# A recurrent attention and low-rank mixer kernel: transposes by the SyncE queue, the low-rank part in the MLP2 bank, two small loads later

## The chip, the cores and the metric

The kernel runs on one core of one Trainium2 chip. A core has TensorE (PE, with its weight loads PEld), VectorE (DVE), ScalarE (ACT), GpSimd (POOL) and SyncE (SP), and 16 DMA engines that work off what the queues hand them. The metric is the device time of one execution in microseconds (us), the median of the runs. The time before is 177.41 us, the median of 3 runs (176.12 to 177.9).

## The reference

For 4 batches of 8 heads, 768 steps and 48 columns a head, a gated recurrence runs over time and its output goes through a low-rank mixing over time and an MLP over the 384 columns:

```python
for t in range(S):
    state = alpha[:, :, t, :, None] * state + np.einsum('bhd,bhe->bhde', k[:, :, t], v[:, :, t])
    y[:, :, t] = np.einsum('bhd,bhde->bhe', q[:, :, t], state)
# x: y with the heads side by side, (batch, 768, 384)
xt = x.transpose(0, 2, 1)
h = xt @ U @ V                      # U: 768 x 32, V: 32 x 768, over time
u = x + h.transpose(0, 2, 1)
ch = np.maximum(u @ w_ch1, 0.0) @ w_ch2      # 384 -> 1536 -> 384
return u + ch
```

Inputs and output are float32; the kernel computes its matmuls in bfloat16.

## The kernel before, in words

Each batch is worked in six units (24 in all, numbered batch*6 + unit). For a unit, four tiles of 128 rows are loaded (alpha, k, q, v, 192 KB each). ScalarE takes the logarithm of alpha (lt), TensorE sums it over time with a triangular matrix (cum, `f_cum`), ScalarE makes exp of the sum and of its negative (aa, ai), and GpSimd or VectorE scales q and k with them (rq, rk, `f_scale`). TensorE transposes rk and rq (`f_tr`) into PSUM, ScalarE or VectorE copies them to SBUF (kT, qT, `f_ev`), TensorE multiplies them (the scores, `f_sc`), VectorE masks (pm), and TensorE makes the unit's y from pm and v and from qT and the state (`f_y`), which is copied into xb. The state itself is built from rk and rv (`f_d`, `f_st`).

Batches 0 and 1 are worked by `stage_pair`, which takes four heads and 256 rows in a unit, batches 2 and 3 by `stage_gla`, which takes all eight heads and 128 rows. Their loads differ too: 128x4x96 (L342) and 128x8x48 (L349), so 512 and 1024 contiguous pieces for the same bytes.

When a batch's xb is there, `stage_mix` multiplies it with U (L681), copies the result (utx), multiplies V with it (L712) and adds xb on VectorE (L713): u, in the tile ub. For the MLP, u has to stand transposed (uT). In batch 0 uT is made straight from xb and utx by L700 and L703 and the copy behind them, and L712 and L713 are done beside it for the last addition alone. In batches 1 to 3 TensorE transposes ub, two row blocks at a time (L722), and one copy brings them to uT.

`mlp1` multiplies uT with w1 (36 matmuls of 384 columns for each half of the batch, L749) and takes the maximum with 0 (L759, L761). `mlp2` multiplies that with w2 in three groups of four matmuls for each of six row blocks (L772), VectorE adds ub (L779), and SyncE stores the 128 rows (L780).

The order of all this is written by a planner, the class `Plan`. Each piece of work is added with its engines and a cost on each, what it reads and writes, and a priority (lower goes first); `run` walks a clock and always gives out the piece that can start first, among those that can start at the same time the one with the lowest priority. From that come each engine's instructions, in a fixed order that the chip follows; each instruction waits for what it needs and holds up what stands behind it in its engine's queue. All loads and stores are issued by SyncE's queue, in such an order too. MLP work has the priority of a unit that lies `LEAD` (3.0) units further on than its batch's end (`mlp_prio`). TensorE works with tiles of different shapes; a piece has a `mode` for it, and the planner adds 95 ns when the mode changes. The eight PSUM banks are a pool (`bank`), and so are the SBUF tiles: 36 for loads (`io`), 4 for rk, 3 for rq, 3 for kT, 4 for qT.

Two small loads, U (L305) and V (L306), are cast by GpSimd and V is spread to four row groups (vm_sb); they have priority 2.5. Until 28 us TensorE also gets matmuls on a tile of zeros (L291) where it has nothing to do.

Of the kernel before, what the change touches and what calls it, by code (L numbers as in the profile page):

```python
# [40 lines left out]
class Plan:  # L41
# [47 lines left out]
    def run(self):  # L89
# [10 lines left out]
        while todo:  # L100
# [79 lines left out]
def kernel(  # L180
# [31 lines left out]

    W2AT = 7.9
    PAIR = (0, 1)
    RES = (1, 1, 1, 0)
    P = Plan()
    nc.scalar.preload_act_table_set("natural_log_exp_and_others")
# [84 lines left out]
            nc.gpsimd.tensor_copy(dst, src)  # L302

    def small():
        P.add({"SP": 450.0}, lambda e: nc.sync.dma_start(u_in, moe_U.rearrange("(c p) r -> p c r", p=128)), w=["u_in"], prio=2.5)  # L305
        P.add({"SP": 500.0}, lambda e: nc.sync.dma_start(v_in, moe_V), w=["v_in"], prio=2.5)  # L306
# [234 lines left out]
    def stage_gla(b, c, sprev, xb):  # L541
# [36 lines left out]
        tk, tq = Buf(bank), Buf(bank)  # L578
        kT, qT = Buf(kts), Buf(qts)

        def f_tr(ring, tb):
            t = bf(tb()).rearrange("p (e c) -> p e c", c=C)
            for p in range(HP):
                nc.tensor.matmul(  # L584
                    t[:, p, :],
                    lhsT=ring()[:, 2 * p : 2 * p + 2, :].rearrange("t h w -> t (h w)"),
                    rhs=ident, start=True, stop=True, is_transpose=True,
                )

        def f_ev(e, dst, tb):  # L590
            copy(e, dst(), bf(tb()).rearrange("p (e c) -> p e c", c=C)[:, 0:HP, :])

        P.add({"PE": mm(*[C] * 4)}, lambda e: f_tr(rk, tk), r=[rk], w=[tk], prio=pr + 18, slack=sl)
        P.add({"PE": mm(*[C] * 4)}, lambda e: f_tr(rq, tq), r=[rq], w=[tq], prio=pr + 18, slack=sl)
        P.add({"DVE": 335, "ACT": 500}, lambda e: f_ev(e, kT, tk), r=[tk], w=[kT], prio=pr + 8, slack=sl)
        P.add({"DVE": 335, "ACT": 500}, lambda e: f_ev(e, qT, tq), r=[tq], w=[qT], prio=pr + 8, slack=sl)

        sc = Buf(bank), Buf(bank)
        pm = Buf(pms)
# [73 lines left out]
    def stage_mix(b, xb, ub, uT):  # L673
# [19 lines left out]
        if b == 0:  # L693
            for tt in range(2):
                tb = [Buf(bank, 2) for _ in range(NCT)]
                cs = range(tt * NT, (tt + 1) * NT)

                def f_x(e, j, tb=tb, cs=cs):
                    for n, c in enumerate(cs):
                        nc.tensor.matmul(tb[j]()[:, n * C : (n + 1) * C], lhsT=xb()[:, c, j * C : (j + 1) * C], rhs=ident, start=(n == 0), stop=False, skip_group_check=True)  # L700

                def f_h(e, j, tt=tt, tb=tb):
                    nc.tensor.matmul(tb[j]()[:, 0:TW], lhsT=utx()[:, j * C : (j + 1) * C], rhs=vm_sb[:, tt * TW : (tt + 1) * TW], start=False, stop=True, skip_group_check=True)  # L703

                for j in range(NCT):
                    P.add({"PE": mm(*[C] * NT)}, lambda e, j=j, f=f_x: f(e, j), r=[x for c in cs for x in xk(b, xb, c)] + [(xb, NC - 2, 0)], w=[tb[j]], prio=pr + tt, slack=sl)
                    P.add({"PE": mm(TW)}, lambda e, j=j, f=f_h: f(e, j), r=[utx, ("vm", tt)], w=[tb[j]], prio=pr + tt, slack=sl)
                    P.add({"ACT": 390, "DVE": 470}, lambda e, j=j, tt=tt, tb=tb: copy(e, uT()[:, j, tt * TW : (tt + 1) * TW], tb[j]()[:, 0:TW]), r=[tb[j]], w=[(uT, tt, j)], prio=pr + tt, slack=sl)
            pr = mlp_prio(0, 0.3)
        for c in range(NC):  # L710
            hb = Buf(bank, 3 if b == 0 else 0)
            P.add({"PE": mm(DM)}, lambda e, c=c, hb=hb: nc.tensor.matmul(hb()[:, 0:DM], lhsT=vm_sb[:, c * C : (c + 1) * C], rhs=utx(), start=True, stop=True), r=[utx, ("vm", c // NT)], w=[hb], prio=pr + c, slack=sl)  # L712
            P.add({"DVE": 465}, lambda e, c=c, hb=hb: nc.vector.tensor_tensor(ub()[:, c, :], xb()[:, c, :], hb()[:, 0:DM], op=ALU.add), r=[hb] + xk(b, xb, c), w=[(ub, c)], prio=pr + c, slack=sl)  # L713
            if c % 2 == 1 and b > 0:
                ub2 = Buf(bank)

                def f_tr(e, c=c, ub2=ub2):
# [13 lines left out]

                P.add({"DVE": 450, "ACT": 710}, f_ev, r=[ub2], w=[(uT, c // 2)], prio=pr + c, slack=sl)

    def mlp_prio(b, x):
        return ((b + 1) * NC + LEAD + x * NC) * 100.0

    def mlp1(b, uT, h1, tt):
        for jt in range(NJ):
# [2 lines left out]

            if b == 0:
                need = [(uT, tt, j) for j in range(NCT)]
            else:
                need = [(uT, 0), (uT, 1)] if tt == 0 else [(uT, 1), (uT, 2)]

# [15 lines left out]

            P.add({"ACT": 395, "DVE": 470}, g, r=[hb], w=[(h1, tt, jt)], prio=-100)

    def mlp2(b, ub, h1, c):
        hb = Buf(bank, RES[b])
        tt = c // NT
        for g in range(3):

            def f(e, g=g):  # L770
                for jt in range(4 * g, 4 * g + 4):
                    nc.tensor.matmul(  # L772
                        hb()[:, 0:DM], lhsT=h1()[:, jt, c * C : (c + 1) * C], rhs=w2_sb[:, jt, :],
                        start=(jt == 0), stop=(jt == NJ - 1),
                    )

            P.add({"PE": mm(*[DM] * 4)}, f, r=[(h1, tt, jt) for jt in range(4 * g, 4 * g + 4)] + [("w2", jt) for jt in range(4 * g, 4 * g + 4)], w=[hb], prio=mlp_prio(b, 0.5 + c / 12.0 + g / 36.0))
        ou = Buf(outs)
        P.add({"DVE": 468}, lambda e: nc.vector.tensor_tensor(ou(), ub()[:, c, :], hb()[:, 0:DM], op=ALU.add), r=[hb, (ub, c)], w=[ou], prio=-100)  # L779
        P.add({"SP": 550.0}, lambda e: nc.sync.dma_start(out[b, c * C : (c + 1) * C, :], ou()), r=[ou], prio=-1)  # L780

    small()
# [4 lines left out]
    for b in range(B):  # L787
        xb, ub, uT, h1 = Buf(xbs), Buf(ubs), Buf(uts), Buf(h1s)
        st = [None, None]
        for c in range(NC):  # L790
            if b in PAIR:
                st[c % 2] = stage_pair(b, c, st[c % 2], xb)
            else:
                st[0] = stage_gla(b, c, st[0], xb)
        stage_mix(b, xb, ub, uT)
        mlp1(b, uT, h1, 0)
        mlp1(b, uT, h1, 1)
        for c in range(NC):
            mlp2(b, ub, h1, c)
    P.run()  # L800
    global PLAN
    PLAN = P
# [30 lines left out]
```

## Time and profile before

| What | Value |
|---|---|
| Time, median of 3 runs | 177.41 us (176.12 to 177.9) |
| The profiled execution's time | 174.75 us |
| Its span, first to last instruction | 173.0 us |
| Granted TensorE clock, mean | 0.986 |
| TensorE busy | 161.9 us (94%), 1862 matmuls |
| VectorE, ScalarE, GpSimd busy | 109.0, 104.1, 59.5 us |
| Moved by DMA | 28.82 MB, 167 GB/s over the span |

Durations in the profile are of one execution, and busy time is the union of an engine's instructions. TensorE's matmuls overlap: the mean of one matmul is longer than the time by which one follows another, so the price of a matmul is read from the chain, where a row says how long a group of them took. A row of the SyncE queue tells how long the queue was held until the next transfer could be issued; the landing comes some us later.

### The profile page before, as it was taken

To read this page: it belongs to the slowest core of one execution; us is meant where nothing else is said; L and a number is where in the kernel's file an instruction comes from. 1 tells how busy PE (TensorE), PEld (TensorE's weight loads), DVE (VectorE), ACT (ScalarE), POOL (GpSimd) and SP (SyncE) were. 2 spreads that over 40 slices of the span, in tenths; PEclk is the share of its full clock that TensorE was granted. 3 is DMA by queue.
4 is the path that set the end of the run, shared out by engine and by line. 5 is a ranking of instruction groups with operands and counts; after the bars stand their busy time and mean duration, and the time that the engine had idled before them with its cause. 6 is when DMAs were issued, how large, how long until landed. Compare 5 with 4: busy or idle time off the path is not lost.

```text
span 173.0 us, 4823 instructions
## 1 busy us (share of the span) xinstructions
PE 161.9 (94%) x1862; PEld 104.2 (60%) x1862; DVE 109.0 (63%) x232; ACT 104.1 (60%) x247; POOL 59.5 (34%) x97
## 2 busy tenths in 40 slices
PE   7688998899996999999998999999999999999991
PEld 2355765566564776676676657666666566656560
DVE  4589685598996986958675559976474294000231
ACT  4588773779785767558949436638783210996000
POOL 8056366247331765255155414910430000000000
PEclk9999699999999999999999999999999999999998
DMA  5999989999998999999989999611000212100222
GB/s 140 266 249 260 267 255 335 258 300 330 269 267 200 178 207 211 214 222 221 230 147 206 189 166 258 170 58 37 0 0 4 91 45 91 51 0 0 91 93 91
DMA packets 83031, 28.82 MB, mean 167 GB/s; under 512 B 76832, under 2 KB 82976, under 8 KB 83008
## 3 DMA queue, kind: packets, MB, share of 16 engines
q1 hardware_dynamic: 83008, 28.52, 72.0%
q8 instruction: 14, 0.23, 0.6%
q14 instruction: 9, 0.07, 0.2%
HBM read 23.79 MB, written 4.72 MB: 165 GB/s over the span
## 4 chain that ended last, share of the span: by engine, by line
PE 60%; DMA 19%; SPq 15%; issue 2%; POOL 1%; ACT 1%; DVE 0%; ACTq 0%; POOLq 0%
PE ps L772 27%; PE ps L749 16%; SPq L342 10%; DMA io<-in_v_dram 8%; DMA io<-in_moe_w_ch_dram 5%; SPq L317 3%; DMA io<-in_alpha_dram 3%; PE ps L584 3%; DMA io<-in_k_dram 3%; PE ps L605 2%; PE ps L712 2%; PE ps L722 2%; PE ps L664 1%; PE ps L554 1%; PE ps L418 1%
## 5 line engine op out<-in xcount | busy, mean ns | idle before, releaser
L749 PE MATMUL ps<-uT,w_sb 128*128 128x384 bf16 x288 | 53.1, 326 | 0.0
L772 PE MATMUL ps<-w_sb,h1t 128*128 128x384 bf16 x288 | 52.8, 326 | 0.0
L759 ACT ACTIVATE h1t<-ps 128x384 bf16<-128x384 f32 x73 | 35.2, 494 | 8.8 <-PE ps L749 8.5
L772 PEld LDWEIGHTS <-h1t 128*128 128x128 bf16 x288 | 26.1, 98 | 16.0 <-issue 1.0
L749 PEld LDWEIGHTS <-w_sb 128*128 128x128 bf16 x288 | 26.1, 98 | 15.4
L779 DVE TENSOR_TENSOR ou<-ub,ps 128x384 f32<-128x384 bf16 x24 | 13.2, 551 | 27.6 <-PE ps L772 27.3
L302 POOL CAST rv<-io 128x384 bf16<-128x384 f32 x19 | 11.2, 590 | 35.7 <-DMA io<-in_v_dram 30.7
L615 DVE TENSOR_TENSOR pm<-ps,maskc 128x512 bf16<-128x512 f32 x24 | 15.7, 685 | 6.7 <-PE ps L605 6.5
L572 POOL TENSOR_TENSOR rk<-io,ai 128x384 bf16<-128x384 f32 x12 | 11.0, 916 | 20.2 <-ACT ai L565 18.7
L761 DVE TENSOR_SCALAR h1t<-ps 128x384 bf16<-128x384 f32 x23 | 12.6, 552 | 7.4 <-PE ps L749 4.8
L456 DVE TENSOR_TENSOR pm<-ps,maskp 128x512 bf16<-128x512 f32 x24 | 15.8, 681 | 0.7 <-ACT h1t L759 0.5
L298 ACT CAST xb<-ps 128x192 bf16<-128x192 f32 (+1 forms) x23 | 8.8, 392 | 11.6 <-PE ps L664 7.6
L298 ACT COPY kt<-ps 128x512 bf16<-128x512 bf16 x17 | 10.0, 586 | 5.8 <-PE ps L584 5.3
L713 DVE TENSOR_TENSOR ub<-xb,ps 128x384 bf16<-128x384 bf16 x24 | 12.1, 547 | 1.2 <-PE ps L712 1.2
L298 ACT COPY qt<-ps 128x512 bf16<-128x512 bf16 x17 | 11.3, 663 | 1.6 <-PE ps L418 1.0
L302 POOL CAST w_sb<-io 128x384 bf16<-128x384 f32 x21 | 10.8, 527 | 3.8 <-DMA io<-in_moe_w_ch_dram 3.5
L572 POOL TENSOR_TENSOR rq<-io,aa 128x384 bf16<-128x384 f32 x12 | 11.6, 967 | 0.0
L375 ACT ACTIVATE lt<-io 128x384 bf16<-128x384 f32 x12 | 6.4, 530 | 5.2 <-DMA io<-in_alpha_dram 5.2
L298 ACT COPY uT<-ps 128x768 bf16<-128x768 bf16 x4 | 3.2, 799 | 8.6 <-PE ps L722 5.1
L547 ACT ACTIVATE lt<-io 128x384 bf16<-128x384 f32 x12 | 6.5, 542 | 2.0 <-DMA io<-in_alpha_dram 2.0
L398 ACT ACTIVATE ai<-ps 128x384 bf16<-128x384 f32 x12 | 5.9, 493 | 2.8 <-PE ps L391 2.8
L565 ACT ACTIVATE ai<-ps 128x384 bf16<-128x384 f32 x12 | 6.0, 500 | 2.4 <-PE ps L557 2.0
(114 smaller groups left out, 249.3 us busy)
## 6 DMA issues: line engine op xcount, KB each, us to landing
io<-in_alpha_dram SPq DMA_DIRECT2D x24, 192.0 KB, 4.3
io<-in_k_dram SPq DMA_DIRECT2D x24, 192.0 KB, 4.5
io<-in_q_dram SPq DMA_DIRECT2D x24, 192.0 KB, 4.3
io<-in_v_dram SPq DMA_DIRECT2D x24, 192.0 KB, 4.5
io<-in_moe_w_ch_dram SPq DMA_DIRECT2D x24, 192.0 KB, 4.4
out_dram<-ou SPq DMA_DIRECT2D x24, 192.0 KB, 1.9
u_in<-in_moe_U_dram SPq DMA_DIRECT2D x1, 96.0 KB, 4.6
v_in<-in_moe_V_dram SPq DMA_DIRECT2D x1, 96.0 KB, 4.3
```

Source lines behind the costliest of these rows:

```text
L298: nc.scalar.copy(dst, src)
L302: nc.gpsimd.tensor_copy(dst, src)
L342: lambda e: nc.sync.dma_start(t().rearrange("p (h j) d -> p h (j d)", j=2), src[b, hs, sl, :].rearrange("h (p j) d -> p h (j d)", j=2)),
L456: nc.vector.tensor_tensor(dst, s2, maskp.to_broadcast([C, 2, 2, C]), op=ALU.mult)
L572: eng.tensor_tensor(dst()[:, :, 0:D], a(), x(), op=ALU.mult)
L615: nc.vector.tensor_tensor(pm()[:, :, par, :], s2, maskc.to_broadcast([C, HP, C]), op=ALU.mult)
L713: P.add({"DVE": 465}, lambda e, c=c, hb=hb: nc.vector.tensor_tensor(ub()[:, c, :], xb()[:, c, :], hb()[:, 0:DM], op=ALU.add), r=[hb] + xk( ...
L749: nc.tensor.matmul(hb()[:, 0:TW], lhsT=w1_sb[:, ct, jt * 128 : (jt + 1) * 128], rhs=uT()[:, ct, tt * TW : (tt + 1) * TW], start=(ct == 0), ...
L759: nc.scalar.activation(dst, hb()[:, 0:TW], AF.Relu)
L761: nc.vector.tensor_scalar_max(dst, hb()[:, 0:TW], 0.0)
L772: nc.tensor.matmul(hb()[:, 0:DM], lhsT=h1()[:, jt, c * C : (c + 1) * C], rhs=w2_sb[:, jt, :], start=(jt == 0), stop=(jt == NJ - 1),)
L779: P.add({"DVE": 468}, lambda e: nc.vector.tensor_tensor(ou(), ub()[:, c, :], hb()[:, 0:DM], op=ALU.add), r=[hb, (ub, c)], w=[ou], prio=-100)
```

## The change

In words:

- In batches 2 and 3 rk and rq are no longer transposed by TensorE. SyncE issues a transposing DMA from the rk or rq tile to the kT or qT tile (`TRD = (2, 3)`), with priority -0.5, so ahead of the loads that are ready at the same time. The transposes' PSUM banks and the two copies fall away.
- In batch 3 each row block of ub is transposed by such a DMA as well (`TRU = (3,)`), one of 128x384 for each of the six row blocks; L722's transposes and their copies remain for batches 1 and 2. `mlp1` then waits for the three row blocks of its half.
- In batch 0 `stage_mix` ends when uT is made. The low-rank product for the last addition is a thirteenth matmul in each row block's MLP2 bank, and the last addition reads xb in place of ub.
- The loads of U and V get priority 4.5 in place of 2.5.
- `LEAD` is 4.0 in place of 3.0, and a piece of TensorE work in another mode than the one before counts as 20 points lower in priority (`STAY`).

```diff
+    STAY = 20.0
-                t1, op = min(((t, o) for t, o in ok if t <= t0 + 1.0), key=lambda x: (x[1].prio, x[1].i))
+                t1, op = min(((t, o) for t, o in ok if t <= t0 + 1.0), key=lambda x: (x[1].prio + (self.STAY if eng == "PE" and x[1].mode != mode else 0.0), x[1].i))
...
+    TRD = (2, 3)
+    TRU = (3,)
...
-        P.add({"SP": 450.0}, lambda e: nc.sync.dma_start(u_in, moe_U.rearrange("(c p) r -> p c r", p=128)), w=["u_in"], prio=2.5)
-        P.add({"SP": 500.0}, lambda e: nc.sync.dma_start(v_in, moe_V), w=["v_in"], prio=2.5)
+        P.add({"SP": 450.0}, lambda e: nc.sync.dma_start(u_in, moe_U.rearrange("(c p) r -> p c r", p=128)), w=["u_in"], prio=4.5)
+        P.add({"SP": 500.0}, lambda e: nc.sync.dma_start(v_in, moe_V), w=["v_in"], prio=4.5)
...
-    LEAD = 3.0
+    LEAD = 4.0
...
+        if b in TRD:
+            for ring, dst in ((rk, kT), (rq, qT)):
+                P.add(
+                    {"SP": 600.0},
+                    lambda e, ring=ring, dst=dst: nc.sync.dma_start(dst(), ring().rearrange("t h w -> t (h w)"), transpose=True),
+                    r=[ring], w=[dst], prio=-0.5,
+                )
+        else:
...
-            pr = mlp_prio(0, 0.3)
+            return utx
...
-            if c % 2 == 1 and b > 0:
+            if b in TRU:
+                P.add(
+                    {"SP": 450.0},
+                    lambda e, c=c: nc.sync.dma_start(uT()[:, :, c * C : (c + 1) * C], ub()[:, c, :], transpose=True),
+                    r=[(ub, c)], w=[(uT, c)], prio=-0.5,
+                )
+            elif c % 2 == 1:
...
+            low = b == 0 and g == 2
...
-                        start=(jt == 0), stop=(jt == NJ - 1),
+                        start=(jt == 0), stop=(jt == NJ - 1 and not low),
...
+                if low:
+                    nc.tensor.matmul(hb()[:, 0:DM], lhsT=vm_sb[:, c * C : (c + 1) * C], rhs=utx(), start=False, stop=True)
...
-        P.add({"DVE": 468}, lambda e: nc.vector.tensor_tensor(ou(), ub()[:, c, :], hb()[:, 0:DM], op=ALU.add), r=[hb, (ub, c)], w=[ou], prio=-100)
+        P.add({"DVE": 468}, lambda e: nc.vector.tensor_tensor(ou(), (xb if b == 0 else ub)()[:, c, :], hb()[:, 0:DM], op=ALU.add), r=[hb] + (xk(b, xb, c) if b == 0 else [(ub, c)]), w=[ou], prio=-100)
```

More of the change, by code (lines that the diff above doesn't have):

```diff
@@ L590, in f_ev, with f_tr @@
[L590 to L596, printed above, removed]
+        if b in TRD:
[4 more added lines that the diff above has]
+                    r=[ring], w=[dst], prio=-0.5,
+                )
+        else:
+            tk, tq = Buf(bank), Buf(bank)
+            def f_tr(ring, tb):
+                t = bf(tb()).rearrange("p (e c) -> p e c", c=C)
+                for p in range(HP):
+                    nc.tensor.matmul(
+                        t[:, p, :],
+                        lhsT=ring()[:, 2 * p : 2 * p + 2, :].rearrange("t h w -> t (h w)"),
+                        rhs=ident, start=True, stop=True, is_transpose=True,
+                    )
+            def f_ev(e, dst, tb):
+                copy(e, dst(), bf(tb()).rearrange("p (e c) -> p e c", c=C)[:, 0:HP, :])
+            P.add({"PE": mm(*[C] * 4)}, lambda e: f_tr(rk, tk), r=[rk], w=[tk], prio=pr + 18, slack=sl)
+            P.add({"PE": mm(*[C] * 4)}, lambda e: f_tr(rq, tq), r=[rq], w=[tq], prio=pr + 18, slack=sl)
+            P.add({"DVE": 335, "ACT": 500}, lambda e: f_ev(e, kT, tk), r=[tk], w=[kT], prio=pr + 8, slack=sl)
+            P.add({"DVE": 335, "ACT": 500}, lambda e: f_ev(e, qT, tq), r=[tq], w=[qT], prio=pr + 8, slack=sl)
@@ L743, in mlp1 @@
                 need = [(uT, tt, j) for j in range(NCT)]
+            elif b in TRU:
+                need = [(uT, c) for c in range(tt * NT, (tt + 1) * NT)]
             else:
```

21 lines of the change are left out of this document (7 added, 14 removed).

## The prediction

> **What bounds the kernel now.** I read the page first, then the engines by stage, then the waits of TensorE, the chain of waits, and last the issue times of the SyncE queue.
>
> ```profile
> span 173.0 us, 4823 instructions
> PE 161.9 (94%) x1862; PEld 104.2 (60%) x1862; DVE 109.0 (63%) x232; ACT 104.1 (60%) x247; POOL 59.5 (34%) x97
> DMA  5999989999998999999989999611000212100222
> PE 60%; DMA 19%; SPq 15%; issue 2%; POOL 1%; ACT 1%; DVE 0%; ACTq 0%; POOLq 0%
> ```
>
> Two resources are full, one after the other in the chain: the DMA engines until slice 25 of 40 (about 108 us), TensorE nearly all the time. A busy TensorE is not proof of a bound, so the stages come next. Columns are the busy time and the instruction count of each engine, then the granted clock, the DMA share and GB/s.
>
> ```profile
> 0.00:36.00 36.00, 30.55 (x441) 19.45 (x442) 24.69 (x67) 24.05 (x59) 17.40 (x40) 0.95 1.03 256
> 56.00:88.00 32.00, 32.00 (x432) 21.63 (x431) 25.21 (x49) 23.22 (x57) 16.67 (x22) 1.00 1.06 210
> 92.00:110.00 18.00, 18.00 (x204) 12.06 (x203) 13.12 (x26) 11.37 (x31) 8.78 (x12) 1.00 1.22 208
> 110.00:146.00 36.00, 36.00 (x352) 23.21 (x350) 22.23 (x41) 16.55 (x37) 6.63 (x8) 1.00 0.13 45
> ```
>
> And what TensorE waited for between 36 and 170 us:
>
> ```profile
> PE ps L479 <- POOL rv L302: 1.5, 1, 1.5
> PE ps L605 <- ACT qt L298: 0.6, 1, 0.6
> ```
>
> So from 36 us on TensorE waits 2.1 us in all, and what leaves its queue there shortens the span; before 36 us the loads set the pace. VectorE and ScalarE are not waited for beyond 0.6 us. The chain of waits gives prices on the bounding engine (start, duration, line and number of instructions):
>
> ```profile
> 63.97 0.45 PE ps L584 x8
> 64.42 0.65 PE ps L772 x4
> ...
> 65.92 0.33 PE ps L605 x8
> 66.25 0.76 PE ps L772 x4
> ...
> 70.63 0.34 PE ps L722 x6
> ...
> 146.10 11.70 PE ps L749 x72
> 157.80 11.71 PE ps L772 x72
> 169.54 0.55 DVE ou L779
> ```
>
> A transpose costs TensorE 0.45/8 = 56 ns (L584) or 0.34/6 = 57 ns (L722). Four MLP2 matmuls take 0.65 us, but 0.76 us behind L605, which uses another tile shape: a change of shape costs 0.11 us. The last batch's MLP is 23.4 us of full-rate matmuls.
>
> **What leaves TensorE.** On TensorE, where the first unit of batch 2 (rk_154, rv_171) is worked, stood in the kernel before:
>
> ```order
> L628 MATMUL ps<-rv_171,rk_154 128x96
> L628 LDWEIGHTS rk_154
> L628 MATMUL ps<-rv_171,rk_154 128x96
> L584 LDWEIGHTS rk_154
> L584 MATMUL ps<-ident,rk_154 128x128
> L584 LDWEIGHTS rk_154
> L584 MATMUL ps<-ident,rk_154 128x128
> ```
>
> and now (L639 is the old L628, L800 the low-rank matmul that joins an MLP2 bank, L521 the old L518 of the unit before):
>
> ```order
> L795 MATMUL ps<-w_sb,h1t_211 128x384
> L800 LDWEIGHTS vm_sb
> L800 MATMUL ps<-utx_206,vm_sb 128x384
> L639 LDWEIGHTS rk_154
> L639 MATMUL ps<-rv_171,rk_154 128x96
> L639 LDWEIGHTS rk_154
> L639 MATMUL ps<-rv_171,rk_154 128x96
> ```
>
> The transposes behind the state matmuls are gone. 12 units x 2 tensors x 4 = 96 transposes at 56 ns are 5.3 us; batch 3's 18 of u at 57 ns are 1.0 us. Batch 0's six low-rank matmuls stay, as L800 in place of L712: nothing. Changes of tile shape fall from 100 to 92 when counted over the order: at most 8 x 0.11 = 0.9 us, part of it in the load-bound start, and I take 0.4. Together 6.7 us off TensorE: span 173.0 - 6.7 = **166.3 us** if nothing new waits.
>
> Off the path, at nothing: 24 copies of kT and qT, 3 copies of uT and 6 additions of u leave ScalarE and VectorE, which are covered by TensorE's work; if that cover were gone, the 0.6 us wait above is what they could give. Batch 0's final addition reads xb where it read ub, at the same price. U and V move behind eight loads:
>
> ```profile
> 8.37 0.68 SPq L305 DMA_DIRECT2D u_in<-in_moe_U_dram  x1
> 9.10 1.05 SPq L306 DMA_DIRECT2D v_in<-in_moe_V_dram  x1
> ...
> L681 PE MATMUL ps<-xb,u_sb x24: 322/336/337, 23.4 to 137.2; 128*32 128x384 bf16 x24
> ```
>
> The eight loads issue 1.7 us earlier, the two small loads near 15 us, 8 us ahead of U's first use at 23.4; what comes behind them keeps its place, so I take nothing (between 0.7 gained and 0.7 lost, the shorter of the two issue times). MLP rows stand one unit further back (LEAD), and the mode bonus reorders a little: same work, and the one place where TensorE waits for a load (L479, 1.5 us) may close or double, so 1.5 either way, taken as nothing.
>
> **What goes into the DMA queue.** 24 transposes of 128 KB and 6 of 96 KB now stand in SyncE's queue. Around the first of them stood before:
>
> ```order
> L780 DMA out_0_dram<-ou0_213 128x384
> L349 DMA io4_116<-in_alpha_dram 128x8x48
> L349 DMA io9_121<-in_k_dram 128x8x48
> L349 DMA io11_123<-in_q_dram 128x8x48
> L349 DMA io6_118<-in_v_dram 128x8x48
> L780 DMA out_0_dram<-ou1_214 128x384
> ```
>
> and now:
>
> ```order
> L352 DMA io9_121<-in_k_dram 128x8x48
> L805 DMA out_0_dram<-ou1_214 128x384
> L352 DMA io11_123<-in_q_dram 128x8x48
> L586 DMA_TRANSPOSE kt0_188<-rk0_154 128x4x128
> L586 DMA_TRANSPOSE qt0_184<-rq0_151 128x4x128
> L352 DMA io6_118<-in_v_dram 128x8x48
> L805 DMA out_0_dram<-ou2_215 128x384
> ```
>
> Each transpose waits on SyncE for GpSimd's rk or rq; behind it queue loads of later units and the outputs, and GpSimd's casts and ScalarE's Ln wait for those. At the end of the loads the queue read, before:
>
> ```order
> L349 DMA io6_118<-in_k_dram 128x8x48
> L780 DMA out_0_dram<-ou3_216 128x384
> L349 DMA io12_124<-in_q_dram 128x8x48
> L349 DMA io15_127<-in_v_dram 128x8x48
> L780 DMA out_0_dram<-ou0_213 128x384
> ```
>
> and now:
>
> ```order
> L586 DMA_TRANSPOSE qt1_185<-rq0_151 128x4x128
> L352 DMA io11_123<-in_q_dram 128x8x48
> L352 DMA io6_118<-in_v_dram 128x8x48
> L586 DMA_TRANSPOSE kt1_189<-rk2_156 128x4x128
> L586 DMA_TRANSPOSE qt2_186<-rq1_152 128x4x128
> L586 DMA_TRANSPOSE kt2_190<-rk3_157 128x4x128
> L586 DMA_TRANSPOSE qt3_187<-rq2_153 128x4x128
> ```
>
> 20 of the 24 transposes now stand ahead of the last load. No row shows such a transpose; its price T on a full queue comes from the queue's own rows (start, time until the next could issue):
>
> ```profile
> 18.98 7.24 SPq L317 DMA_DIRECT2D io<-in_moe_w_ch_dram  x12
> ...
> 39.99 1.25 SPq L342 DMA_DIRECT2D io<-in_k_dram  x1
> ...
> 53.27 0.57 SPq L349 DMA_DIRECT2D io<-in_alpha_dram  x1
> ...
> 61.72 1.07 SPq L780 DMA_DIRECT2D out_dram<-ou  x1
> ...
> 105.29 0.64 SPq L780 DMA_DIRECT2D out_dram<-ou  x1
> ...
> 106.50 0.69 SPq L349 DMA_DIRECT2D io<-in_v_dram  x1
> ```
>
> All these move 192 KB. Weights, 128 rows of 384 numbers, take 7.24/12 = 0.60 us. The sixteen loads from 39.99 to 53.27 come in 512 pieces (128x4x96): 0.83 us. From 53.27 to 107.19 there are 48 loads in 1024 pieces (128x8x48) and 8 outputs (61.72 to 105.29); with the outputs at the weights' 0.60, a load is (53.92 - 4.8)/48 = 1.02 us. By the first and the last of these a piece costs 0.42 us/896 = 0.47 ns and the bytes alone 0.54 us (for the middle one that makes 0.78, measured 0.83). A transpose moves two thirds of the bytes and writes 128x4 pieces of 256 bytes: 0.36 + 512 x 0.47 ns = **0.60 us, an estimate**. The lower end is 128 pieces, 0.42 us; the upper end, as long as a whole L349 load, 1.02 us. I take 0.60, since its piece count is that of the middle rows.
>
> The Trainium skill speaks against the change here: "VectorE: DVE Perf Modes", section "The three transpose paths", gives a 128x128 transpose 390 ns on TensorE and 1309 ns by DMA, and advises TensorE where PSUM will do. The chain's 56 ns already undercuts the first figure; by the second, four blocks in turn would be an estimated 5.2 us and 20 of them some 92 us more.
>
> With T = 0.60 the issue of the last load, which ended at 106.50 + 0.69 = 107.19, ends at 107.19 + 4 more outputs x 0.60 + 20 x 0.60 = 121.6 us. From there the shortest way to the end has these rows, of the last unit and the last mix before:
>
> ```profile
> DMA to landing us min/median/max: 3.2/4.2/5.5
> ...
> out_dram<-ou SPq DMA_DIRECT2D x24, 192.0 KB, 1.9
> ...
> 128.92 0.91 POOL L572 TENSOR_TENSOR rq<-io,aa 128x384 bf16<-128x384 f32 x1
> ...
> 132.31 0.40 PE L605 MATMUL ps<-qt,kt 48*128 48x128 bf16 x8
> ...
> 135.41 0.36 PE L664 MATMUL ps<-rv,pm 128*128 128x48 bf16 x8
> ...
> 137.01 0.50 PE L681 MATMUL ps<-xb,u_sb 128*32 128x384 bf16 x6
> ...
> 138.75 1.14 PE L712 MATMUL ps<-utx,vm_sb 128*128 128x384 bf16 x6
> 139.12 2.41 DVE L713 TENSOR_TENSOR ub<-xb,ps 128x384 bf16<-128x384 bf16 x5 [0.26 <-PE ps L712]
> ```
>
> Before, the last rq ran at 128.92, some 18 us after its load: the loads had slack. Now: issued 120.9 + 4.2 landing = 125.1; rq 0.9 and a gap of 0.1: 126.1; its transpose on a queue that has run empty 1.9 + 0.6 = 2.5: 128.6; L605 to L664 3.1, to L681 1.6, to L712 1.7 as in the rows: 135.0; three additions of u (0.4 until the first starts, then 3 x 0.5): 136.9; transpose of the third row 1.9 + 0.45 (384 pieces, half the bytes): 139.3; and from the start of the last MLP1 to the end as before, 173.0 - 146.10 = 26.9: **166.2 us**. Both paths end together, so a little is lost where they meet. Before, one wait for qt cost 0.6; now every unit has such a wait through the queue. I add two of these, 1.2 us (bounds 0 and, at a third of a us in each of 12 units, 4). Span **167.5 us**.
>
> **The rivals.** *The queue becomes the bound, slower.* Each 0.05 us on T moves the end by 1.0 us. The change is lost at span 173.0, T = 0.60 + 5.5/20 = 0.88; it is over 1% slower from T = 0.97. At 1.02 the span is 166.2 + 8.4 + 1.2 = 175.8 us. For it: DMA is full until 108 us, and no row shows a transpose. Against: its bytes and pieces are fewer than an L349 load's. 0.15.
>
> *Four transfers in one, much slower.* If the queue works each 128-column block as a transfer of its own, at the 0.60 us of the shortest transfer in the rows, T is 2.4 and the span 167.5 + 20 x 1.8 = 203.5 us. Nothing in the trace speaks for it but that no such transfer is in it. The page on VectorE named above would put it higher still. 0.04.
>
> *The gain turns into waits.* With T between 0.79 and 0.97, or 4 us of waits at the units, loads arrive just as TensorE has run out of MLP rows, and the span is 171.2 to 174.8. 0.14.
>
> *The waits that are there go too.* If T is at the lower end, the loads reach the end 3.6 us earlier, and with the 2.1 us of waits gone and the whole 0.9 us of shape changes won the span is 166.3 - 2.1 - 0.5 = 163.7 us. 0.07.
>
> **How the numbers follow.** My forecast has 0.60, which leaves 0.67 for faster by over 1%. The profiled execution took 174.75 us, 1.75 beyond its span and 2.66 below the median of 177.41; I keep both distances, so a span s stands for s + 4.4. Forecast: 167.5 gives 169.25 profiled and **171.9 us**. The range runs from the third rival, 163.7 (168.1), to T = 1.02, 175.8 (180.2). 1% of 177.41 is 1.8 us, about what a measurement of this kernel can tell from no change: 175.6 and 179.2 are the spans 171.2 and 174.8 used above.
>
> **What would show it.** L584 gone, L739 (the old L722) at 36 matmuls; TensorE's waits from 36 us on near 3 us, for kt and qt landing; the last L352 load issued near 121 us rather than 106.5; a transpose of 0.6 us in a full queue, landing in 4.2 us there and about 2.5 at the end; the last MLP1 starting near 140 us. Wrong if the last load issues after 127 us, or if TensorE stands idle ahead of L616 for over 0.5 us per unit.

## The result, and the profile after

The changed kernel is slower: 182.72 us (median of four runs, 181.11 to 183.44) against 176.76 us (175.75 to 177.9) for the kernel before on the same chip, a ratio of 1.032 with a 95% interval of 1.022 to 1.042. The forecast was 171.9 us, its range ended at 180.2: the sign was wrong, and the range did not hold the time. Some executions of a kernel take over 1.5% longer than its fastest; the ratios leave them out, the medians do not. The profiled execution of the changed kernel took 182.83 us, of which the span is 181.0; before it was 173.0, so 8.0 us are to be found.

The page of the changed kernel begins like this; the last line is the DMA queue (packets, MB, share of 16 engines).

```profile
span 181.0 us, 4585 instructions
PE 157.2 (87%) x1746; PEld 98.7 (55%) x1749; DVE 102.1 (56%) x215; ACT 93.8 (52%) x223; POOL 62.2 (34%) x105
DMA  4999999999999997899899998998889314410222
PE 39%; DMA 28%; SPq 17%; POOL 5%; ACT 4%; issue 3%; DVE 2%; POOLq 0%; ACTq 0%; DVEq 0%
q1 hardware_dynamic: 98560, 32.26, 84.1%
```

The instructions did leave TensorE: 1862 recorded matmuls became 1746 and its busy time fell by 4.7 us. But the DMA engines, empty from about 108 us on before, are now busy until slice 31 of 40 (140 us), and in the chain TensorE's share fell from 60% to 39% while DMA rose from 19% to 28%. TensorE's waits of the changed kernel between 36 and 178 us (line waited for: us in total, times, longest) say where the saving went:

```profile
PE ps L616 <- DMA qt<-rq: 4.7, 8, 1.2
PE ps L557 <- ACT lt L550: 4.5, 6, 1.5
PE ps L639 <- POOL rv L305: 1.6, 3, 0.7
PE ps L770 <- DMA uT<-ub: 1.6, 1, 1.6
PE ps L616 <- ACT h1t L780: 0.6, 1, 0.6
```

These are 13.0 us where there were 2.1. Two kinds stand out: the score matmuls (L616) wait for the transposed q, and the cumulative sums (L557) wait for ScalarE's Ln of alpha. The second is a late load. In the waits of all engines, ScalarE's wait for alpha's load was 2.0 us in the kernel before (first row) and is 17.2 in the changed one (second row):

```profile
ACT lt L547 <- DMA io<-in_alpha_dram: 2.0, 4, 1.4
```

```profile
ACT lt L550 <- DMA io<-in_alpha_dram: 17.2, 12, 3.7
```

What made the loads late is seen in the SyncE queue of the changed kernel (start, duration, line and operation). A duration here is the time for which the instruction holds SyncE's queue, not the time until the data has landed:

```profile
69.64 0.57 SPq L352 DMA_DIRECT2D io<-in_v_dram  x1
70.31 0.53 SPq L805 DMA_DIRECT2D out_dram<-ou  x1
70.94 1.24 SPq L586 DMA_TRANSPOSE kt<-rk  x1
72.27 1.22 SPq L586 DMA_TRANSPOSE qt<-rq  x1
...
133.53 0.57 SPq L352 DMA_DIRECT2D io<-in_v_dram  x1
136.91 1.21 SPq L586 DMA_TRANSPOSE kt<-rk  x1
138.21 1.22 SPq L586 DMA_TRANSPOSE qt<-rq  x1
```

The same by source, with the time from issue to landing of L586 (durations in ns, min/median/max):

```profile
L586 SPq DMA_TRANSPOSE kt<-rk x12: 1205/1242/2456, 65.8 to 136.9; - x12
L586 SPq DMA_TRANSPOSE qt<-rq x12: 1205/1214/1370, 68.4 to 138.2; - x12
...
DMA to landing us min/median/max: 2.4/3.3/5.4
...
L728 SPq DMA_TRANSPOSE uT<-ub x6: 1183/1206/1215, 149.1 to 157.0; - x6
```

A transposing instruction holds the queue for 1.2 us. It is the same at 70.94 in a full queue and at 136.91, when the last load has gone out and only transposes stand ahead; and the same for the 96 KB of L728 as for the 128 KB of L586. The load and the output shown beside it hold the queue 0.57 and 0.53 us. The 20 transposes ahead of the last load hold it 26.6 us in all by their rows, of which 20 x 1.21 = 24.2 are this hold, so waiting in the queue for GpSimd's rk and rq can be 2.4 us of it at most. The last load is issued by 133.53 + 0.57 = 134.1 us, where it was 107.19 before and 121.6 was forecast.

### The profile page after: what moved, and what is told of

Its sections match the earlier page's. It is cut to its first block, busy times and chain, and to the rows that moved or that the text cites. A ratio compares the mean times of both kernels' runs of the same rounds, so it can differ in the third digit from the quotient of the medians.

```text
span 181.0 us, 4585 instructions
## 1 busy us (share of the span) xinstructions
PE 157.2 (87%) x1746; PEld 98.7 (55%) x1749; DVE 102.1 (56%) x215; ACT 93.8 (52%) x223; POOL 62.2 (34%) x105
## 4 chain that ended last, share of the span: by engine, by line
PE 39%; DMA 28%; SPq 17%; POOL 5%; ACT 4%; issue 3%; DVE 2%; POOLq 0%; ACTq 0%; DVEq 0%
PE ps L770 16%; PE ps L795 13%; DMA io<-in_alpha_dram 11%; SPq L345 9%; DMA io<-in_v_dram 4%; DMA qt<-rq 4%; SPq L586 4%; DMA io<-in_q_dram 4%; DMA io<-in_moe_w_ch_dram 2%; POOL rk L575 2%; SPq L320 1%; PE ps L421 1%; POOL rv L305 1%; POOL rq L575 1%; SPq L352 1%
## 5 line engine op out<-in xcount | busy, mean ns | idle before, releaser
L770 PE MATMUL ps<-uT,w_sb 128*128 128x384 bf16 x288 | 51.8, 328 | 1.6 <-DMA uT<-ub 1.6
L804 DVE TENSOR_TENSOR ou<-ub,ps 128x384 f32<-128x384 bf16 x18 | 10.0, 554 | 30.5 <-PE ps L795 30.2
L305 POOL CAST rv<-io 128x384 bf16<-128x384 f32 x23 | 11.9, 518 | 29.2 <-DMA io<-in_v_dram 19.3
L550 ACT ACTIVATE lt<-io 128x384 bf16<-128x384 f32 x12 | 6.3, 523 | 17.2 <-DMA io<-in_alpha_dram 17.2
L301 ACT CAST xb<-ps 128x192 bf16<-128x192 f32 (+1 forms) x20 | 7.7, 387 | 12.9 <-PE ps L675 10.2
L616 PE MATMUL ps<-qt,kt 48*128 48x128 bf16 x96 | 4.8, 217 | 5.3 <-DMA qt<-rq 4.7
L724 DVE TENSOR_TENSOR ub<-xb,ps 128x384 bf16<-128x384 bf16 x18 | 8.7, 548 | 0.3 <-PE ps L723 0.3
L301 ACT COPY uT<-ps 128x768 bf16<-128x768 bf16 x5 | 4.0, 799 | 9.2 <-PE ps L739 5.4
L557 PE MATMUL ps<-lt,ut_ones 128*128 128x384 bf16 x12 | 4.0, 337 | 4.5 <-ACT lt L550 4.5
L616 PEld LDWEIGHTS <-kt 48*128 48x128 bf16 x96 | 3.3, 93 | 7.6 <-issue 4.1
L568 ACT ACTIVATE ai<-ps 128x384 bf16<-128x384 f32 x12 | 5.9, 495 | 2.7 <-PE ps L560 2.4
```

Source lines behind the costliest of these rows:

```text
L301: nc.scalar.copy(dst, src)
L770: nc.tensor.matmul(hb()[:, 0:TW], lhsT=w1_sb[:, ct, jt * 128 : (jt + 1) * 128], rhs=uT()[:, ct, tt * TW : (tt + 1) * TW], start=(ct == 0), ...
```

## The experiments

The two theories after the result: *the hold* (every transposing instruction costs SyncE's queue some 1.2 us, however little it moves, and with 20 of them ahead of the last load the loads become the bound) and *the engines* (the transposed bytes and pieces themselves are slow in the DMA engines). Beside them stood the other parts of the change, and the planner, which counted 600 ns for such a transfer. Ratios are against the kernel before on the same chip, with a 95% interval.

**The price by itself.** Behind the last output of the kernel before, 24 transfers from SBUF to SBUF, each waiting for the one before it through its buffer, so that the queue and the engines are empty:

```diff
     P.run()
+    for n in (1, 2, 3, 4, 8):
+        for _ in range(3):
+            nc.sync.dma_start(dst[:, 0:n*C].rearrange("p (n c) -> p n c", c=C), src[:, 0:n*C], transpose=True)
+    for n in (1, 4, 8):
+        for _ in range(3):
+            nc.sync.dma_start(dst[:, 0:n*C], src[:, 0:n*C])
```

> The kernel before with 24 transfers from SBUF to SBUF added behind its last output, when the queue is empty: transposing ones of 128, 256, 384, 512 and 1024 columns, three of each, then plain copies of 128, 512 and 1024 columns, three of each. Its total time means nothing; the spacing of the transfers does. Theory of the instruction (a transposing transfer holds the SyncE queue for a time of its own, whatever it moves): spacing near 1.2 us at 128 to 512 columns, as the 1.21 us of the changed kernel at 384 and 512, and little more at 1024. Theory of the bytes (the time goes with blocks moved): 0.3 us at 128 columns, 1.2 at 512, 2.4 at 1024. Plain copies: near 0.4 us.

The queue of this kernel, one of each of three sizes (128, 512 and 1024 columns) and one plain copy of 512 columns, and the groups by source:

```profile
175.37 1.09 SPq L805 DMA_TRANSPOSE uT<-h1t  x1
...
196.41 1.19 SPq L805 DMA_TRANSPOSE uT<-h1t  x1
204.99 1.23 SPq L805 DMA_TRANSPOSE uT<-h1t  x1
217.29 0.46 SPq L808 DMA_DIRECT2D uT<-h1t  x1
...
L805 SPq DMA_TRANSPOSE uT<-h1t x15: 1095/1186/1232, 170.7 to 205.0; - x15
...
L808 SPq DMA_DIRECT2D uT<-h1t x9: 464/465/546, 208.0 to 223.8; - x9
```

And what the same transfers took of the DMA engines: stretches that hold three of one size each (the last two columns are the DMA share and GB/s), transposes of 512 and of 1024 columns, then plain copies of 512 and of 1024.

```profile
191.53:198.84 7.31, 0.00 (x0) 0.00 (x0) 0.00 (x0) 0.00 (x0) 0.00 (x0) 0.50 0.28 54
198.84:208.04 9.20, 0.00 (x0) 0.00 (x0) 0.00 (x0) 0.00 (x0) 0.00 (x0) 0.50 0.46 86
213.35:219.25 5.90, 0.00 (x0) 0.00 (x0) 0.00 (x0) 0.00 (x0) 0.00 (x0) 0.50 0.20 67
219.25:226.00 6.75, 0.00 (x0) 0.00 (x0) 0.00 (x0) 0.00 (x0) 0.00 (x0) 0.50 0.31 117
```

The three transposes of 128 columns hold the queue 1.19, 1.10 and 1.09 us. Eight times the columns lengthen the hold to 1.23; it is a price per instruction. The engines' time does go with the size: 7.31 x 0.28 / 3 = 0.68 us for 512 columns and 9.20 x 0.46 / 3 = 1.41 us for 1024, against 0.39 and 0.70 for the copies. So the forecast's 0.60 was near the engines' price of such a transfer, and the price on the queue is another one, about twice as large.

**Only the transposes left out.** The changed kernel with q and k transposed on TensorE again, everything else of the change kept:

```diff
-    TRD = (2, 3)
+    TRD = ()
```

> The changed kernel with q and k of batches 2 and 3 back on TensorE, all else of the change kept. If the 24 transposing transfers are the cause: last load issued near 107 us instead of 133.5, TensorE's waits from 36 us on back to 2 to 5 us from 13.0, time 174 to 177 us, 0.95 to 0.97 of the changed kernel. If the new priorities (LEAD, STAY) are the cause: it stays near 182 us with waits for lt and rv.

Measured: 174.78 us, ratio 0.998 (0.992 to 1.004), span 173.8, and the last load is back at 109.5 us. The loss is gone with these 24 instructions.

**Only the transposes put in.** The kernel before with that one block:

```diff
+    TRD = (2, 3)
...
+        if b in TRD:
+            for ring, dst in ((rk, kT), (rq, qT)):
+                P.add({"SP": 600.0}, lambda e, ring=ring, dst=dst: nc.sync.dma_start(dst(), ring().rearrange("t h w -> t (h w)"), transpose=True), r=[ring], w=[dst], prio=-0.5)
```

> The kernel before with the transposing transfers of q and k in batches 2 and 3 alone. If they are the cause: 180 to 185 us, the last load issued near 130 us. If the priorities are the cause: 171 to 174 us, since 5.3 us leave TensorE and nothing is added to it.

Measured: 182.98 us, ratio 1.045 (1.027 to 1.064). The queue and TensorE's waits of this kernel:

```profile
131.74 0.53 SPq L350 DMA_DIRECT2D io<-in_v_dram  x1
```

```profile
PE ps L614 <- DMA qt<-rq: 6.5, 9, 1.2
```

The transposes alone bring the whole loss, with the last load at 132 us. Both runs agree with either theory; they clear the rest of the change.

**The rest alone.** Neither q, k nor u through the queue; the low-rank part in MLP2's bank, the late U and V and the changed order stay:

```diff
-    TRD = (2, 3)
-    TRU = (3,)
+    TRD = ()
+    TRU = ()
```

> The change without any transposing transfer: the low-rank part in the MLP2 bank, U and V late, LEAD 4 and STAY 20 alone. TensorE's work is the same but for changes of shape, so 0 to 1 us below the kernel before: 0.990 to 1.003 of it. If the priorities cost waits of their own: 1.005 or more.

Measured: 175.17 us, ratio 1.002 (0.999 to 1.006). These parts are worth nothing that can be measured.

**Half as many instructions for the same bytes.** In the changed kernel rk and rq of a unit are put side by side in one tile, kT and qT as well, and one transpose of 1024 columns takes the place of two of 512:

```diff
-    rq_s = slots("rq", 3, [C, H, 64], BF16)
-    rk_s = slots("rk", 4, [C, H, 64], BF16)
+    rkq_s = slots("rkq", 4, [C, 2, H, 64], BF16)
...
-            for ring, dst in ((rk, kT), (rq, qT)):
-                P.add(
-                    {"SP": 600.0},
-                    lambda e, ring=ring, dst=dst: nc.sync.dma_start(dst(), ring().rearrange("t h w -> t (h w)"), transpose=True),
-                    r=[ring], w=[dst], prio=-0.5,
-                )
+            P.add(
+                {"SP": 1200.0},
+                lambda e: nc.sync.dma_start(KQ(), RR().rearrange("t x h w -> t (x h w)"), transpose=True),
+                r=[rkk, rqk], w=[kTk, qTk], prio=-0.5,
+            )
```

> The changed kernel with rk and rq side by side in one tile, and kT and qT too, so that one transposing transfer of 1024 columns does for both: 12 instead of 24, the same bytes and pieces. Theory of the instruction: 10 of them ahead of the last load instead of 20 save some 12 us of the queue, last load near 121 us, time 171 to 176 us. Theory of the bytes: the last load stays near 133 us and the time near 182.

Measured: 175.8 us, ratio 1.001 (0.993 to 1.009). Its queue, the group by source, and TensorE's wait for the transposed u:

```profile
125.47 0.80 SPq L351 DMA_DIRECT2D io<-in_v_dram  x1
...
L592 SPq DMA_TRANSPOSE kqt<-rkq x12: 1232/1788/2848, 68.9 to 130.3; - x12
```

```profile
PE ps L776 <- DMA uT<-ub: 2.1, 1, 2.1
```

SyncE's own waits ahead of these transposes, by the same columns:

```profile
SPq L592 <- POOL rkq L580: 11.1, 7, 2.5
```

With the same bytes in the same 256-byte pieces the last load goes out 7.8 us earlier (126.3 against 134.1) and nearly the whole loss is gone. This is the run that speaks most clearly between the two theories: the engines need 2 x 0.68 = 1.36 us for two transposes of 512 columns and 1.41 for one of 1024, so had their time alone been the bound, halving the instructions would have changed nothing. The rows agree: the 20 holds add up to 26.6 us, these 10 to 19.4, which is 7.2 us less. But it is not the 12 us less that the hold alone, at 1.23 a transfer, would have given, and the last load came 5 us later than the 121 expected. What lengthened the hold to a median of 1.79 was not settled: a joined transpose waits for both rk and rq, and SyncE's waits name GpSimd's scaling (L580) for 11.1 us; the engines' 1.41 us is the other candidate.

One thing stays open. While the holds delay the loads the DMA engines do not fall idle: their busy share in the changed kernel is 1.10 from 65.8 to 108.9 us and 0.92 from there to 134.1, against 1.13 from 65.8 to 107 us before. The 48 loads, too, take 39.0 us of the queue by their rows where they took 40.3 before, so the holds come almost wholly on top. Why the engines do not make up for them afterwards, no row shows. The joined run also has a buffer more for rq and for kT, which was not tried apart.

**The joined transpose without u's.** The same, and batch 3's u stays on TensorE:

```diff
-    TRU = (3,)
+    TRU = ()
```

> Joined transposing transfers in batches 2 and 3, u of batch 3 on TensorE again. Against the joined kernel that transposes u by transfer it gives TensorE 1.0 us more work and takes away its wait of 2.1 us for uT: 0 to 2 us less, 173 to 176 us.

Measured: 173.07 us, ratio 0.988 (0.984 to 0.993): faster than the kernel before, and so than the changed one. Its page, its queue and TensorE's waits from 36 us on:

```profile
span 169.6 us, 4598 instructions
PE 155.4 (92%) x1764; PEld 98.2 (58%) x1767; DVE 101.3 (60%) x214; ACT 96.7 (57%) x228; POOL 61.8 (36%) x105
...
122.53 0.78 SPq L351 DMA_DIRECT2D io<-in_v_dram  x1
```

```profile
PE ps L645 <- POOL rv L304: 1.8, 3, 0.8
PE ps L560 <- ACT lt L553: 0.9, 2, 0.7
PE ps L622 <- DMA kqt<-rkq: 0.8, 1, 0.8
```

Here the TensorE time that was taken out does shorten the span. The issue of the last load ends at 123.3 us, within 2 us of where the forecast put it, and the span is 169.6.

**The joined transpose for one batch.** Batch 2 back on TensorE, u too:

```diff
-    TRD = (2, 3)
-    TRU = (3,)
+    TRD = (3,)
+    TRU = ()
```

> Joined transposing transfers (1024 columns, one for q and k) in batch 3 alone; batch 2 and u of batch 3 on TensorE. Half the transposes leave TensorE (48 x 56 ns = 2.7 us), and 3 or 4 transfers of 1.25 us stand ahead of the last load, which goes out near 113 us. Theory of the instruction: 171 to 175 us, a little below the kernel before. If even few such transfers hurt: 177 us or more.

Measured: 174.32 us, ratio 0.998 (0.993 to 1.002), last load at 110.4. The loads are hardly later than before, but only half of TensorE's saving (48 transposes, 2.7 us) is there to be had, and no gain that can be measured is left of it.

**Single transposes for one batch.** The same edit on the changed kernel with its two transposes per unit:

> Transposing transfers of q and k singly in batch 3 alone, batch 2 and u on TensorE: 12 transfers, 8 of them ahead of the last load. Theory of the instruction: 8 x 1.24 = 10 us later than 107, last load near 117 to 119 us; TensorE has 2.7 us less to do; time 174 to 178 us, above the joined one with 6 transfers (174.3).

Measured: 177.67 us, ratio 1.009 (1.005 to 1.013), last load at 114.7. It has twelve transposes where the joined form has six, and is about 1% slower. The last load alone does not explain it, since in the run of copies below a later one costs nothing. The last transpose is issued at 132.07 us, but the profiled execution was the longest of this kernel, so where the loss falls was not settled.

**The same transfers with nobody waiting.** The kernel before, with all its transposes on TensorE, and 24 transfers more, from rk and rq into three spare tiles that nothing reads; once transposing, once as plain copies:

```diff
+        for ring in (rk, rq):
+            sp = Buf(spares)
+            P.add({"SP": 600.0}, lambda e, ring=ring, sp=sp: nc.sync.dma_start(sp(), ring().rearrange("t h w -> t (h w)"), transpose=True), r=[ring], w=[sp], prio=-0.5)
```

> The kernel before, with TensorE's transposes kept, and the 24 transposing transfers of rk and rq added to the SyncE queue at the same priority, into spare tiles that nobody reads. TensorE gains nothing and waits for none of them. If the queue's lateness is the harm (loads behind the transfers come late): last load issued beyond 125 us, waits of 8 us or more for lt, rv and rk, time 180 to 188 us. If the harm is that TensorE waits for kT and qT to land: within 2% of the kernel before, below 178 us.

> The same with plain copies of 128x512 numbers in place of the transposing transfers: the same bytes, 0.46 us of issue instead of 1.2, 0.39 us of the DMA engines instead of 0.68. Theory of the instruction: the last load is issued near 117 us, time at most 2% above the kernel before (174 to 178 us). If any 24 more transfers of these bytes do the harm: as with the transposing ones, 180 us or more.

Measured: 183.89 us, ratio 1.048 (1.044 to 1.053), for the transposing ones, and 176.13 us, ratio 1.003 (0.999 to 1.006), for the copies. The queue and the groups of the first and of the second kernel:

```profile
133.46 0.42 SPq L350 DMA_DIRECT2D io<-in_v_dram  x1
...
L601 SPq DMA_TRANSPOSE spare<-rk x12: 1189/1266/1842, 68.0 to 138.6; - x12
```

```profile
121.16 0.45 SPq L350 DMA_DIRECT2D io<-in_v_dram  x1
...
L601 SPq DMA_DIRECT2D spare<-rk x12: 465/527/1309, 68.5 to 130.2; - x12
```

The transposing ones lose as much as the change lost, and more, though no matmul waits for them: late loads cost without TensorE waiting for kT and qT. The copies put the last load 14.4 us later (121.6 against 107.19) and cost nothing, so the loads had at least that much slack, as the forecast assumed. That is 4.6 us later than the 117 expected: less 2.4 us for the four outputs that moved ahead, a copy cost 0.60 us, more than its 0.46 us of issue and its 0.39 us of the engines. The pair does not part the hold from the engines by itself, since the transposes also come in nearly four times as many packets; the joined run bears on that. And the first kernel's whole loss is not the loads' alone: its granted clock was 0.963, against 0.986 in the profile of before.

**Issued by ScalarE.** The single transposes on ScalarE's queue, u on TensorE:

```diff
-                    {"SP": 600.0},
-                    lambda e, ring=ring, dst=dst: nc.sync.dma_start(dst(), ...
+                    {"ACT": 1250.0},
+                    lambda e, ring=ring, dst=dst: nc.scalar.dma_start(dst(), ...
```

> The changed kernel with the 24 transposing transfers of q and k issued from ScalarE's queue instead of SyncE's; u of batch 3 is transposed by TensorE again, so that one queue alone transposes; the planner counts 1.25 us of ScalarE for each and 2.4 us more until it has landed. If what is short is the SyncE queue's time of issue: the last load is issued near 108 us, ScalarE is held 24 x 1.2 = 29 us, time 170 to 177 us. If the DMA engines themselves are slowed by such transfers, whoever issues them: the last load stays beyond 125 us, time 180 us or more.

Measured: 186.31 us, ratio 1.059 (1.050 to 1.069). The first row is the group by source, the second the last load, the others are from SyncE's waits:

```profile
L587 ACTq DMA_TRANSPOSE kt<-rk x12: 1206/1207/1346, 62.3 to 139.1; - x12
```

```profile
128.15 0.37 SPq L353 DMA_DIRECT2D io<-in_v_dram  x1
```

```profile
SPq L806 <- DVE ou L805: 45.4, 13, 13.2
SPq L353 <- DMA qt<-rq: 14.9, 7, 4.8
```

The hold follows the instruction to whichever engine issues it: 1.21 us, now taken from ScalarE. With SyncE freed of it the loads still did not flow: the issue of the last one ends at 128.5 us and the time is over 180 us, the two signs that were set down for the engines. But it does not decide for them, since SyncE's loads waited for other things: 14.9 us for transposes that ScalarE had issued, and outputs 45.4 us for VectorE's results (13 waits over the whole span) with loads behind some of them. A load needs nothing from a transpose; the landings in this trace are marked by eight semaphores that all transfers share, which may be the reason, but that was not tried. So this run neither shows nor excludes that such transfers slow the engines whoever issues them, and what another queue would give without these waits stays open.

**The planner told the price.** The changed kernel, with 1250 ns in place of 600 for the two transposes, so that the planner orders the queue by what they take:

```diff
-                    {"SP": 600.0},
+                    {"SP": 1250.0},
```

> The changed kernel with the planner told 1250 in place of 600 for a transposing transfer of q or k; nothing else. If it is the planner's wrong price that makes TensorE wait (rows for late tiles put too early): waits from 36 us on fall from 13 us below 6 and the time to 174 to 178 us. If the queue's time itself is the bound: last load still issued near 130 us, time 180 us or more.

Measured: 185.81 us, ratio 1.053 (1.042 to 1.064), last load at 135.9. TensorE's wait for q's transposes fell from 4.7 to 0.8 us, and the time did not get better. Its profile has a granted clock of 0.96, which may account for some of that; but the loads came as late as in the changed kernel (134.1, at a clock of 0.991). Spacing the queue by the price of q's and k's transposes did not help (the six of u kept their 450 ns): the loads stay behind the same 20 transposes.

Put side by side by the end of the last load, most kernels with a late one fall on one line:

| kernel | issue of the last load ends | span | between |
|---|---|---|---|
| joined, u on TensorE | 123.3 | 169.6 | 46.3 |
| joined | 126.3 | 174.0 | 47.7 |
| transposes alone | 132.3 | 179.2 | 46.9 |
| nobody waiting, transposing | 133.9 | 182.6 | 48.7 |
| changed kernel | 134.1 | 181.0 | 46.9 |
| planner told the price | 135.9 | 184.0 | 48.1 |
| issued by ScalarE | 128.5 | 186.1 | 57.6 |
| nobody waiting, copies | 121.6 | 174.2 | 52.6 |
| the rest alone | 107.9 | 173.3 | 65.4 |

In the first six rows 46 to 49 us of work follow the last load. The last two lie off that line, their loads early enough not to decide. The run on ScalarE's queue lies off it too, with a late load and 57.6 us behind it: there TensorE's waits for q's transposes alone are 9.6 us.

## Why the prediction was wrong

**The step that failed** is the price T: "its price T on a full queue comes from the queue's own rows", and the 0.60 us that came of them by bytes and pieces. The rows that priced it were plain transfers, whose hold of the queue (0.53 to 0.57 us in the changed kernel's rows above) lies below the 1.02 us that the forecast read for a load, so that the rows of a full queue do not show what an instruction holds it by itself. A transposing instruction is the other way round: 0.68 us of the engines at 512 columns, 1.19 us of the queue. Bytes and pieces gave the first, nearly rightly, and say nothing of the second. The upper end failed with it: "as long as a whole L349 load, 1.02 us" was a bound only if bytes and pieces set the price. A row that does not exist in the trace cannot be bounded from above by the rows of other operations, and that end set the end of the range. The split had a smaller slip besides: the eight outputs held 8.3 us by their rows before, not the 4.8 taken, so that a load is (53.92 - 8.3)/48 = 0.95 us and the same working gives 0.57 for T; it changes nothing.

**What the rest of the sum gives with the measured price.** With T = 1.24 the forecast's own formula puts the end of the last load at 107.19 + 2.4 + 20 x 1.24 = 134.4 us (measured 134.1), and the span at 166.2 + 20 x 0.64 + 1.2 = 180.2 (measured 181.0). So the mechanism, the count of 20 and, but for some 2 us, the path behind the last load were right; a term of 12 us was sized at half. That the first sum comes so close is partly luck: by their rows the 20 transposes took 26.6 us rather than 24.8, and the loads 1.3 us less than before. "Each 0.05 us on T moves the end by 1.0 us" fits the joined kernel as well: its transposes hold 7.2 us less and its last load ends 7.8 us earlier.

**The path to the end, step by step.** These rows of the changed kernel's timeline answer to those of the forecast:

```profile
136.33 0.91 POOL L575 TENSOR_TENSOR rq<-io,aa 128x384 bf16<-128x384 f32 x1 [1.39 <-DMA io<-in_q_dram]
...
142.39 0.40 PE L616 MATMUL ps<-qt,kt 48*128 48x128 bf16 x8 [0.74 <-DMA qt<-rq]
...
148.19 1.14 PE L723 MATMUL ps<-utx,vm_sb 128*128 128x384 bf16 x6
...
154.17 6.01 PE L770 MATMUL ps<-uT,w_sb 128*128 128x384 bf16 x36 [1.59 <-DMA uT<-ub]
```

From the end of the last load's issue to L616 it takes 8.3 us (134.1 to 142.39), where the forecast had 128.6 - 121.6 = 7.0: rq is done 3.1 us behind the load and not 4.5, since it needs q's load, which goes out one before the last; but its transpose stands 1.0 us behind kT's in the queue, and L616 starts 4.2 us after it was issued, where the forecast had 2.5 for "a queue that has run empty". From L616 to L723 it takes 5.8 us, where the rows of before gave 6.4. From L723 to the last MLP1 it takes 5.98 us where the forecast had 1.9 + 2.4 = 4.3: the transposes of u's three tiles hold the queue 1.2 us each, one behind the other, and I had charged the last one 0.45. From there to the end it takes 26.8 us, as forecast (26.9). Together the path is 46.9 us, forecast 44.6 and 1.2 more for waits.

**TensorE's saving, 6.7 us.** (96 transposes at 56 ns are 5.4 us rather than 5.3, which changes nothing.) Real, but not what sets the end of the changed kernel. It is seen in the joined kernel without u's transposes: 6.5 us less busy time (155.4 against 161.9) and a span 3.4 us shorter; of the 3.1 us between, 1.8 are waits (3.9 us in all where there were 2.1). The two profiles differ in granted clock, 1.00 against 0.986; by the medians on that chip, 173.07 against 175.42, the gain is 2.4 us. Putting q and k back on TensorE takes the loss away, and takes this gain away too.

**The waits added at the units, 1.2 us.** Too few: TensorE waited 4.7 us in eight places for q's transposes. It is probably a part of the same bound and not a second loss, since the transposes that nobody waits for lost as much; the two were not parted further. I had put the sign "if TensorE stands idle ahead of L616 for over 0.5 us per unit" among those that would prove me wrong; by this row it stood 4.7/12 = 0.4, while the other sign, the last load after 127 us, came true by 7 us.

**What was costed at nothing.** The late U and V, the low-rank part in MLP2's bank and the moved order were rightly costed: the run with these alone has the ratio 1.002 (0.999 to 1.006). The transposes of u were costed as a gain of 1.0 us; between the two joined kernels they lose some: a wait of 2.1 us ahead of the last MLP1, and a ratio of 1.001 against 0.988, measured on two chips, with intervals that just meet.

**The rivals.** "The queue becomes the bound, slower" was what happened, by its own mechanism and place; it had 0.15, and its price of 175.8 us for the span was too small because it ended at 1.02. "Four transfers in one" did not happen: a transfer of four or eight blocks holds the queue hardly longer than one of a single block. Here the Trainium skill's "VectorE: DVE Perf Modes", section "The three transpose paths", was near and I read it wrongly: its 1309 ns for a transposing transfer of 128x128 stands beside a measured hold of 1.09 to 1.19 us, but it is not a price per block. Taken as the price per instruction, its estimate would have been 167.5 + 20 x (1.31 - 0.60) = 181.7 us for the span, against 181.0 measured. I had weighed it as per block or not at all.

**What is left.** The span grew by 8.0 us. The path through the last load, with the measured T in it, accounts for it to within a microsecond. Counted along TensorE instead, 173.0 - 6.7 + 10.9 more in waits make 177.2; the other 3.8 us stand in no row of the matmuls' waits. Weight loads waited 3.3 us for kT, and the granted clock was 0.95 between 64 and 100 us where it was 1.00 before; how the two share the rest was not tried.

## What to carry to other kernels

An instruction in a DMA queue has two prices, its hold of the issuing queue and its time in the DMA engines, and in a full queue here each added transfer, transposing or plain, cost at least the larger of the two. Rows of plain loads tell nothing of another operation's hold, so an operation with no row of its own deserves one small measurement, or a range that reaches well past its neighbours. A transposing transfer of 128 to 1024 columns held the queue about 1.1 to 1.2 us, so make few large ones: joining two per unit, with u's transposes left on TensorE, turned this change from 3% slower to 1% faster. And ask how much later the loads may come before the engines notice: here 14 us cost nothing, and some 27 us cost 8.

## What the runs showed of the hardware

A transposing transfer between tiles in SBUF holds its issuing queue 1.09 to 1.19 us at 128 columns and 1.23 us at 1024, on an empty queue, where a plain copy takes 0.46; ScalarE's queue shows the same 1.21 us. What the queue does in that time no row shows. The Trainium skill, "DMA: Bandwidth & Descriptors", section "Issuing engines are not separate DMA queues", holds that the time an engine spends on issuing is usually small beside the transfer itself. The price run does not agree where the transfer is taken as its time in the engines: at 512 columns a transpose has 1.19 us of issue against 0.68, a plain copy 0.46 against 0.39. Taken from issue to landing, a transpose is 2.2 to 3.1 us and a copy 1.7 to 2.3, so that the transposes' issue is still over a third of it.

In the engines a transposing transfer takes about twice the time of a copy of the same bytes: 0.68 against 0.39 us for 128 KB and 1.41 against 0.70 for 256 KB.

In the changed kernel a stretch in which TensorE often stood idle has a lower granted clock. Stretch from 64 to 100 us, the kernel before and then the changed one (busy time of PE, PEld, DVE, ACT and POOL, clock, DMA share, GB/s):

```profile
64.00:100.00 36.00, 35.37 (x412) 23.87 (x410) 24.81 (x48) 24.88 (x60) 15.96 (x21) 1.00 1.14 206
```

```profile
64.00:100.00 36.00, 30.59 (x298) 18.64 (x293) 19.01 (x37) 18.14 (x43) 13.53 (x19) 0.95 1.08 172
```

The 5.4 us of idle time come with a clock of 0.95. How much idle time there is does not settle the clock: in the same stretch the joined kernel has 3.4 us of it at 1.00, the kernel with the transposes alone 3.3 us at 0.91. What does was not tried.
